# A linear-attention and FFN kernel on one core: all FFN2 pairs as seven block products, key-weight sums folded on TensorE, and a new order of parts

## The chip, the cores and the metric

The kernel runs on one core of a Trainium2 chip. Its time is the device time of one execution in microseconds (us). PE is TensorE, DVE is VectorE, ACT is ScalarE, POOL is GpSimd, and SP is SyncE, whose queue issues nearly all the DMAs of this kernel.

## The reference

All data are float32. x is 2048 x 512, there are 32 heads of 16, and the FFN is 1792 wide.

```python
x  = A_x
xn = _layernorm(x)                                  # no scale, no shift, eps 1e-5
q, k, v = split_heads(xn @ wqkv)
phi = lambda u: concat(softmax(u @ w_phi), softmax(-(u @ w_phi)))   # per head, 16 -> 32
kv  = einsum("bhsf,bhsd->bhfd", phi(k), v);  z = phi(k).sum(over s)
o   = einsum(phi(q), kv) / (einsum(phi(q), z) + 1e-6)
s   = o @ wo
g   = silu(mish(xn @ w1 + b1) @ w2)
out = x + s * g
```

## The kernel before

**How it is ordered.** The kernel is written as named parts, and a table ORDER lists them: a letter for the kind of part and a number for its chunk. Running the parts only records operations, each with the engines that may do it and a price for each engine. `simulate`, a planner in Python that runs when the kernel is built, then places the recorded operations one after the other on DVE (V), POOL (G), ACT (A) and SP's queue (Q), by data, by free buffers of a pool and by prices; PE's operations stay in the order in which the parts recorded them. The chosen order is then issued by one helper, `issue`, so nearly every instruction of the trace carries its line (L372 before), and groups are told apart by their tiles. An `either` operation may go to DVE or POOL. The planner also counts a shared memory port of DVE and POOL (`port`), and it prices a DMA by its bytes over DRATE.

**How products are made.** Every float32 operand is split into a high and a low part of a rounded type (`split`: the high part is a rounding copy, the low part the difference), and a product is three matmuls: low by high, high by low, high by high. Large products are cut into 2 x 2 blocks and made by seven block products instead of eight, from sums and differences of blocks.

**Stages, in about the order of time.** `fold` multiplies the key and query weights by the per-head map w_phi: 4 matmuls of 128x128 for each of the 4 chunks of 128 rows (tiles wkf and wqf), which the profile shows as 8 records. `weights_k` and `weights_s` build the seven block operands of the joint key and value weights (wv0, wv1, wk, ws1 to ws4). Part N (`norm`) loads one tile of 128 rows of x, forms its mean and variance on DVE, adds eps, takes the power -1/2 on POOL (tile rs), scales, transposes on PE (tile pt) and writes the block operands (tiles fh, fl, xs, xc). Ka to Kd are the four parts of the seven key and value products of a chunk pair (banks kx, ky, kz); the value tiles are four fixed buffers v0 to v3, and A adds phi(k) v into kvp. Q makes the queries, D and U the quotient, O the product with wo. P splits one w1 block and writes it to DRAM (w1d), M loads it back (w1b), and L loads the block operands of the second half of the tokens (fh, fl from xd; 14 transfers of 512 KB). Fa to Fd are the seven products of FFN1 for one pair of 128 columns and half of the tokens; their outputs ha to hd go to DRAM (hd). R prepares w2. G (`ffn2`, `act`) is FFN2: for each T of eight groups of 256 tokens and each b of seven pairs of hidden chunks it loads the hidden block (tile r), takes Mish on ACT, splits it (ah, al) and adds its products into the banks y. For b under DIRECT = 2 that product is made directly: 12 matmuls of 512 columns, or in the last group 24 of 256. For b = 2 to 6 the block sums (three operations on r) come first, the split is of 128x896 instead of 128x512, and the product is 21 matmuls of 256 columns. E (`final`) joins the banks of a T (tile yy), takes Silu, and multiplies and adds s and x.

PE may use eight PSUM banks. The pools that the change touches: `s2` (11 buffers of 128x512: x, k, ha to hd, r and its splits for b under DIRECT, xx, sr), `slot` (38 of 128x1024) and `rq`.

Of the kernel before, what the change touches and what calls it, by code (L numbers as in the profile page):

```python
# [17 lines left out]
P = 128  # L18
# [15 lines left out]
SLOTS, S2 = 38,11  # L34
SLACK, AHEAD, LAT = 15000, 40000, 150
WAKE, NEAR = 13, 2500
ORDER = """
wk0 N6 N0 wv1 N1 wk1 wv0 N2 Ka0 Ka1 N3 ws Kb0 N7 b1 Kc0 N4 Kd0 wq0 wq1 N5 Kb1 P0 Kc1 Fa0 Kd1 A0 Ka2 Kb2 Kc2 Fb0 N8 N9
N10 Kd2 A1 Ka3 Kb3 Fc0 Kc3 N11 Kd3 N12 P5 A2 Ka4 Fd0 Kb4 Fa5 Fb5 Kc4 A3 N14 P4 Ka5 Fc5 Kd4 Kb5 Kc5 Fd5 N13 Fa4 Kd5 Fb4
A4 Fc4 N15 Ka6 Kb6 A5 Ka7 Kc6 Kb7 P3 P2 P6 Kc7 Kd7 Fa6 Kd6 Fa3 Fa2 Fb3 wQ Fb6 M0 Fc3 Fc6 Fd4 A6 P1 A7 Fa1 Fb2 Fd3 Q0  # L40
Fd6 Fc2 z D0 Fb1 Fc1 D1 L Q3 Q1 D2 Q2 Fa7 D3 Fb7 Fd1 Fd2 D4 M1 Q4 M3 Fc7 Fa10 Fd7 Fa8 D5 Fb8 D6 Fc8 M2 Fd8 D7 Fb10 Q7
M6 Fa9 D8 M5 Fc10 M4 Fb9 Q5 Fd10 Fc9 Q6 D9 Fa13 Fd9 Fa12 D10 Ub0 Fb13 Fb12 D11 Fc13 Fc12 D12 wo0 Fa11 wo1 Fb11 D13 Ua0
D14 Fc11 Fd13 O1 O4 O6 O7 R1 O0 O3 O5 R2 R0 Fd11 Fd12 G7 D15 Ua1 R4 G8 O2 Ub1 G14 G15 R5 O9 O15 O10 O8 G9 G16 R3 G17
G10 G11 R6 G12 G18 G19 G13 E1 G0 O14 G1 G20 E2 G2 O13 G3 G4 O11 G28 G5 G29 G30 G6 G31 G32 G33 G34 G35 E0 G21 G36 G22
G23 G24 E4 G37 G38 G39 G40 G41 G25 G42 G26 O12 E5 G27 G43 G44 G45 G49 E3 G46 G50 G47 G48 G51 E6 E7
# [8 lines left out]
class Program:  # L54
# [105 lines left out]
    def links(self):  # L160
        ops = self.ops
        wr, rd = {}, {}
        for o in ops:
            o.succ, dep = [], set()
# [27 lines left out]
    def simulate(self, at):  # L192
# [22 lines left out]
        dma = port = told = 0  # L215
# [25 lines left out]
        def go(o, e):  # L241
            nonlocal aset, dma, port, half, code, fetched, cold
# [31 lines left out]
            if e == "Q":  # L274
                if not lanes:
                    dur = 0
                    busy[e] = now
                nb = calls[0][1][0].free_size() * calls[0][1][0].shape[0] * 4
                dma = max(dma, now + (1100 if now > 2500 else 1350)) + nb / DRATE
                end = max(dma + 1000, now + 2000 + nb / 200)  # L280
                lanes.append(end)
                heapq.heappush(events, (dma - BACK, 2, -1))
# [16 lines left out]
        while left:  # L299
# [34 lines left out]
            for e in ("A", "V", "G", "Q"):  # L334
# [3 lines left out]
                while ready[e]:  # L338
# [4 lines left out]
                    if e in o.lock and port > now + PTOL:  # L343
# [16 lines left out]
                if held and port > told:  # L360
                    told = port
                    heapq.heappush(events, (port, 2, -1))
# [40 lines left out]
def block_kernel(ctx: ExitStack, tc: tile.TileContext, x, wqkT, wv, phi, wo, w1, b1, w2, out):  # L403
# [9 lines left out]
    for tag, n in (("slot", SLOTS), ("s2", S2), ("sm", 13), ("rq", 5), ("st", 3 * NT), ("tq", 2)):  # L413
        pools[tag] = ctx.enter_context(tc.tile_pool(name=tag, bufs=n))
        prog.cap[tag] = n
# [52 lines left out]
    mhalf = const.tile([P, 1], F32, name="mhalf")  # L468
    b1t = const.tile([P, FC], F32, name="b1t")
    bmask = const.tile([P, 8], F32, name="bmask")  # L470
    vb = [const.tile([P, D], F32, name=f"v{i}") for i in range(4)]
# [68 lines left out]

    def norm(t):
        xx = load_x(t)
        st = sm([P, 6], f"st{t}")
        V.bn_stats(st, xx)
        mv = alloc("st", [P, 2], f"mv{t}")
        V.bn_aggr(mv, st)
        rs = alloc("st", [P, 1], f"rs{t}")
        V.tensor_scalar(rs, mv[:, 1:2], 1e-5, None, op0=ALU.add)
        G.tensor_tensor(rs, rs, mhalf, op=ALU.pow)
        nb = alloc("st", [P, 1], f"nb{t}")  # L550
        V.tensor_scalar(nb, mv[:, 0:1], rs, -1.0, op0=ALU.mult, op1=ALU.mult)
        with one():
            V.tensor_scalar(xx, xx, mv[:, 0:1], rs, op0=ALU.subtract, op1=ALU.mult)
# [69 lines left out]
    ek, eq, rq, phT, oT, kv = {}, {}, {}, {}, {}, {}  # L623
# [10 lines left out]
    def kv_a(c):  # L634
        x, z, v0 = bank([P, D], f"kx{c}"), bank([P, D], f"kz{c}"), vb[2 * c % 4]
# [6 lines left out]
    def kv_b(c):  # L642
        x, y, v1, k1 = kv[c], bank([P, D], f"ky{c}"), vb[(2 * c + 1) % 4], s2(f"k{2 * c + 1}p")
# [6 lines left out]
    def kv_c(c):  # L650
# [5 lines left out]
        plus(vb[(2 * c + 1) % 4], y)  # L656
# [36 lines left out]
    def kv_acc(p):  # L693
# [101 lines left out]
    def prep2(b):  # L795
# [5 lines left out]
        if b < NB - 2:  # L801
            th, tl, eh, el = (slot([P, n, 2 * P], f"w2{m}{b}", F32R) for m, n in (("h", 4), ("l", 4), ("g", 3), ("m", 3)))
        else:
            w = alloc("tq", [P, 16, 2 * P], f"w2t{b}", F32R)
            th, tl, eh, el = w[:, 0:4], w[:, 4:8], w[:, 8:11], w[:, 11:14]
# [6 lines left out]
        split(e, eh, el, either)  # L812
        w2_[b] = [(th[:, i], tl[:, i]) for i in range(4)] + [(eh[:, i], el[:, i]) for i in range(3)]
# [120 lines left out]
    def final(T):  # L934
        y = lambda n: ys[T][HOME[T == NQ - 1][n][0]][:, HOME[T == NQ - 1][n][1], :]
        plus_ = lambda o, a, b: V.tensor_tensor(o, a, b, op=ALU.add)
        if T < NQ - 1:
# [13 lines left out]
            for i in range(2):  # L951
                t = token(T, 1 - i)
                xx, st = s2(f"xx{t}"), s2(f"sr{t}")
                Q.dma_start(xx, x[t * P:(t + 1) * P, :])
                Q.dma_start(st, sdram[t])
                either(st, u[:, i], st, op=ALU.mult)
                either(xx, st, xx, op=ALU.add)
                Q.dma_start(out[t * P:(t + 1) * P, :], xx)
# [23 lines left out]

    w = {"o": [None] * KC}
# [65 lines left out]
    def sums():  # L1049
# [16 lines left out]
        for i in range(4):  # L1066
# [46 lines left out]
```

## Time and profile before

| | |
|---|---|
| median of 3 runs | 501.36 us (500.89 to 501.74) |
| profiled execution, its own time | 501.55 us |
| its span, first to last instruction | 499.8 us |
| mean granted clock of TensorE | 0.991 |
| PE busy | 487.7 us, 98% |
| DVE busy | 443.6 us, 89% |
| ACT busy | 282.4 us, 57% |
| POOL busy | 271.1 us, 54% |
| DMA | 105.69 MB, mean 211 GB/s |

Busy time of an engine is given over the span. Matmuls are pipelined, so one is listed with 0.39 us where the next starts 0.23 us later: a step from start to start is what a matmul costs in a full row.

### The profile page before, as it was taken

How to read it: one execution, taken by the hardware profiler on the slowest of the kernel's cores; microseconds unless marked ns; L12 is line 12 of the kernel's file. 1: busy time of each engine (PE TensorE's matmuls, PEld its weight loads, DVE VectorE, ACT ScalarE, POOL GpSimd, SP SyncE). 2: the span in 40 equal slices, each digit the busy share in tenths (PEclk: the TensorE clock that was granted, in tenths of full speed). 3: DMA queues.
4: the chain of work that ended last, by engine and by line, in shares of the span. 5: the costliest groups of instructions: out<-in, count | busy, mean ns of one | idle time of the engine just before them, and what ended most of it. 6: DMA issues, size and time to landing. Idle time of an engine off the chain costs nothing.

```text
span 499.8 us, 10023 instructions
## 1 busy us (share of the span) xinstructions
PE 487.7 (98%) x3690; PEld 424.3 (85%) x3690; DVE 443.6 (89%) x830; ACT 282.4 (57%) x433; POOL 271.1 (54%) x204
## 2 busy tenths in 40 slices
PE   8699999999999999999999999999999999999996
PEld 8478888878888889888898878778998899999996
DVE  6989999989999999999999989989587899768875
ACT  4676666445365552535243664487356888758611
POOL 4669997689688154889559497643020312112200
PEclk9799999999999999999999999999999999999999
DMA  8524438646979879888766286462644846644742
GB/s 303 185 92 161 148 97 297 220 190 171 358 287 321 298 257 337 306 274 285 251 216 231 100 289 225 170 211 94 201 133 148 269 150 191 207 150 139 255 154 85
DMA packets 68641, 105.69 MB, mean 211 GB/s; under 512 B 6896, under 2 KB 37744, under 8 KB 68592
## 3 DMA queue, kind: packets, MB, share of 16 engines
q1 hardware_dynamic: 68448, 104.79, 62.1%
q8 instruction: 29, 0.48, 0.4%
q10 hardware_dynamic: 144, 0.26, 0.2%
q14 instruction: 20, 0.16, 0.1%
HBM read 60.60 MB, written 44.43 MB: 210 GB/s over the span
## 4 chain that ended last, share of the span: by engine, by line
PE 91%; DVE 6%; ACT 2%; issue 1%; DMA 0%; DVEq 0%; ACTq 0%
PE y L372 28%; PE fx L372 15%; PE pw L372 9%; PE kx L372 8%; PE fy L372 7%; PE qx L372 5%; PE ky L372 4%; PE fz L372 4%; PE qy L372 2%; PE pn L372 2%; PE kz L372 2%; PE kvp L372 1%; PE pt L372 1%; PE qz L372 1%; PE wake L372 1%; PE wqf L372 1%
## 5 line engine op out<-in xcount | busy, mean ns | idle before, releaser
L372 POOL TENSOR_TENSOR r<-r 128x128 f32<-128x128 f32 (+1 forms) x18 | 10.2, 576 | 95.3 <-DVE r L372 56.6
L372 ACT ACTIVATE ah<-r 128x896 fp32r<-128x896 f32 (+1 forms) x56 | 46.8, 854 | 18.0 <-DVE r L372 9.4
L372 DVE TENSOR_TENSOR al<-r,ah 128x896 fp32r<-128x896 f32 (+1 forms) x45 | 46.3, 1047 | 9.1 <-ACT ah L372 4.9
L372 DVE TENSOR_TENSOR r<-r 128x128 f32<-128x128 f32 (+1 forms) x102 | 36.2, 384 | 6.8 <-ACT r L372 5.1
L372 ACT ACTIVATE r<-r 128x512 f32<-128x512 f32 x56 | 34.1, 624 | 14.1 <-DMA r<-hd 12.4
L372 PE MATMUL y<-w2t,ah 128*128 128x256 f32 x224 | 41.0, 283 | 0.0
L372 PE MATMUL fx<-fh,w1b 128*128 128x512 f32 x112 | 38.5, 392 | 0.0
L372 PEld LDWEIGHTS y<-w2t,ah 128*128 128x128 f32 x224 | 34.9, 192 | 0.2
L372 PE MATMUL y<-w2t,al 128*128 128x256 f32 x112 | 31.7, 283 | 0.0
L372 POOL TENSOR_TENSOR al<-r,ah 128x896 fp32r<-128x896 f32 (+1 forms) x11 | 20.1, 1829 | 21.0 <-ACT ah L372 9.5
L372 PE MATMUL y<-w2h,ah 128*128 128x256 f32 x96 | 27.2, 283 | 0.0
L372 PE MATMUL y<-w2l,ah 128*128 128x256 f32 x96 | 27.2, 283 | 0.0
L372 PE MATMUL y<-w2h,al 128*128 128x256 f32 x96 | 27.1, 283 | 0.0
L372 PEld LDWEIGHTS fx<-fh,w1b 128*128 128x128 f32 x112 | 21.0, 188 | 5.0 <-DVE ha L372 0.4
L372 PE MATMUL fx<-fl,w1b 128*128 128x512 f32 x56 | 21.9, 390 | 0.0
L372 PEld LDWEIGHTS y<-w2t,al 128*128 128x128 f32 x112 | 21.5, 192 | 0.2
L372 ACT ACT_TABLE_LOAD x13 | 16.7, 1283 | 6.9 <-DVE yy L372 5.5
L372 PE MATMUL y<-w2g,al 128*128 128x256 f32 x72 | 20.4, 283 | 0.0
L372 PE MATMUL y<-w2m,ah 128*128 128x256 f32 x72 | 20.4, 283 | 0.0
L372 PE MATMUL y<-w2g,ah 128*128 128x256 f32 x72 | 20.4, 283 | 0.0
L372 PE MATMUL fy<-fh,w1b 128*128 128x512 f32 x56 | 19.5, 389 | 0.0
L372 ACT ACTIVATE hb<-fx,b1t 128x512 f32<-128x512 f32 x14 | 9.6, 689 | 17.0 <-PE fx L372 14.5
(735 smaller groups left out, 1837.8 us busy)
## 6 DMA issues: line engine op xcount, KB each, us to landing
r<-hd SPq DMA_DIRECT2D x56, 256.0 KB, 3.5
xd<-xc SPq DMA_DIRECT2D x8, 896.0 KB, 5.5
w1b<-w1d SPq DMA_DIRECT2D x14, 512.0 KB, 4.6
w1b<-w1d SPq DMA_DIRECT2D x14, 384.0 KB, 4.3
so<-so SPq DMA_DIRECT2D x16, 256.0 KB, 2.6
x<-x SPq DMA_DIRECT2D x15, 256.0 KB, 4.0
w1a<-w SPq DMA_DIRECT2D x7, 512.0 KB, 5.4
w1d<-w1sh SPq DMA_DIRECT2D x7, 512.0 KB, 2.8
```

Of the source, the lines that this page charges most:

```text
L372: ins = getattr(e, m)(*a, **k)
```

## The change

- **FFN2.** DIRECT goes from 2 to 0, so that b = 0 and 1 take the path of the seven block products in all eight groups T. Their hidden blocks move from pool s2 to pool slot. For b = 0 to 4 one of the two weight tiles is laid out anew, one of its halves in s2.
- **Key weights.** Before, wkr kept the fold of chunks 0 and 1, and DVE added the fold of chunks 2 and 3 to it. Now `sum_k` folds chunk 0 and chunk 2 into one bank (and 1 and 3 into another), which is the sum; `low_k` folds chunks 2 and 3 and splits them at once; `diff_k` folds 0 and 1 and subtracts them from the value weights; `last_k` makes the fourth sum. Eight chunk folds stand where four stood.
- **Layer norm.** From tile 2 on, eps and power are taken once for two tiles (`stats`), so the first of a pair waits for the second's statistics.
- **Buffers.** The value tiles come from s2, which grows from 11 to 15 buffers; rq grows from 5 to 8.
- **Output.** The last multiplication and addition of `final` become a part of their own, H.
- **Planner.** One port clock for DVE and another for POOL, with a gap of GUARD = 140 behind DVE; PEN goes from -1000 to 0; DRATE from 300 to 400, with more for short runs; NEAR from 2500 to 4000; an operation also follows the first one on the same pooled tile.
- **Order.** ORDER is written anew.

```diff
-DIRECT = 2
+DIRECT = 0
-PEN, HOLD, MARGIN, PTOL = -1000, 300, 1000, 0
-BACK, COLD, DRATE, LANES, SWITCH = 1500, 3400, 300, 8, 300
+PEN, HOLD, MARGIN, GUARD = 0, 300, 1000, 140
+BACK, COLD, DRATE, LANES, SWITCH = 1500, 3400, 400, 8, 300
-SLOTS, S2 = 38,11
+SLOTS, S2 = 38,15
 ORDER = """
-wk0 N6 N0 wv1 N1 wk1 wv0 N2 Ka0 Ka1 N3 ws Kb0 N7 b1 Kc0 N4 Kd0 wq0 wq1 N5 Kb1 P0 Kc1 Fa0 Kd1 A0 Ka2 Kb2 Kc2 Fb0 N8 N9
+N0 kl wv1 wv0 kd N2 N1 N8 Ka1 wq0 N3 Ka4 ks N9 N6 k4 N7 Ka0 N4 Kb0 N5 Kc0 Kd0 Ka3 Kb1 N10 Kc1 P0 N11 Kb3 Kd1 Ka5 b1
...
-    def fold(wT, name, c):
-        ps = bank([P, D], f"{name}f{c}")
+    def fold(wT, name, *cs):
+        ps = bank([P, D], f"{name}f{cs[0]}{len(cs)}")
         with one():
-            for g in range(KC):
-                PE.matmul(ps[:, g * P:(g + 1) * P], wT[c][:, g, :], phit[:, g, :], start=True, stop=True)
+            for c in cs:
+                for g in range(KC):
+                    PE.matmul(ps[:, g * P:(g + 1) * P], wT[c][:, g, :], phit[:, g, :], start=c == cs[0] and g == 0,
+                              stop=c == cs[-1] and g == KC - 1, skip_group_check=True)
...
+    def stats(ts):
+        n = len(ts)
+        rs = alloc("st", [P, n], f"rs{ts[0]}")
+        mv = alloc("st", [P, n, 2], f"mv{ts[0]}")
+        for i, t in enumerate(ts):
+            xx = load_x(t)
+            st = sm([P, 6], f"st{t}")
+            V.bn_stats(st, xx)
+            V.bn_aggr(mv[:, i], st)
+            xs_[t] = xx, mv[:, i, 0:1], rs[:, i:i + 1]
+        V.tensor_scalar(rs, mv[:, :, 1], 1e-5, None, op0=ALU.add)
+        G.tensor_tensor(rs, rs, mhalf[:, 0:n], op=ALU.pow)
...
-        x, z, v0 = bank([P, D], f"kx{c}"), bank([P, D], f"kz{c}"), vb[2 * c % 4]
+        x, z = bank([P, D], f"kx{c}"), bank([P, D], f"kz{c}")
+        v0 = vs[2 * c] = s2(f"v{2 * c}")
...
-            ps = fold(wkT, "wk", 2 + j)
-            V.tensor_tensor(s[:, j], wraw["k"][:, j], ps, op=ALU.add)
-            split(ps, hi[:, j], lo[:, j])
...
+    def sum_k():
+        wraw["s"], wkv[3] = slot([P, 2, D], "ws2"), halves("ws", 1)
         for j in range(2):
+            ps = fold(wkT, "wk", j, j + 2)
+            V.tensor_tensor(wraw["s"][:, j], ps, wraw["v", 0][:, j], op=ALU.subtract)
+            split(ps, *(t[:, j] for t in wkv[3]))
+        wkv[4] = split_raw(wraw["s"], "ws2")
+    def low_k():
+        wkv[2] = halves("wk", 1)
+        for j in range(2):
+            split(fold(wkT, "wk", 2 + j), *(t[:, j] for t in wkv[2]))
```

PE at the start of the program. Before, the first folds come first, and the products kx and kz of two chunk pairs follow (x is a tile of the input, pt its transpose, wkf a fold):

```order
L372 MATMUL wake<-ones 128x128 x13
L372 MATMUL wkf_144<-phit,wkT_139 128x128 x4
L372 MATMUL wkf_145<-phit,wkT_140 128x128 x4
L372 MATMUL pt_151<-ident,x_146 128x128 x4
L372 MATMUL pt_157<-ident,x_152 128x128 x4
L372 MATMUL pt_166<-ident,x_161 128x128 x4
L372 MATMUL wkf_172<-phit,wkT_141 128x128 x4
L372 MATMUL wkf_173<-phit,wkT_142 128x128 x4
L372 MATMUL pt_182<-ident,x_177 128x128 x4
L372 MATMUL kx_183<-wv0h,fl_106 128x512
L372 MATMUL kx_183<-wv0l,fh_105 128x512
```

In the changed kernel:

```order
L371 MATMUL wake<-ones 128x128 x13
L371 MATMUL pt_144<-ident,x_141 128x128 x4
L371 MATMUL wkf_147<-phit,wkT_137 128x128 x4
L371 MATMUL wkf_148<-phit,wkT_138 128x128 x4
L371 MATMUL wkf_156<-phit,wkT_135 128x128 x4
L371 MATMUL wkf_157<-phit,wkT_136 128x128 x4
L371 MATMUL pt_167<-ident,x_162 128x128 x4
L371 MATMUL pt_173<-ident,x_170 128x128 x4
L371 MATMUL pt_183<-ident,x_178 128x128 x4
L371 MATMUL kx_185<-wv0h,fl_102 128x512
```

The four folds that stood apart now stand together behind one transpose. Further down, behind the products of two chunk pairs and two query folds, PE has the summed folds, two transposes whose x comes late, and then the third pair:

```order
L371 MATMUL wkf_202<-phit,wkT_135 128x128 x4
L371 MATMUL wkf_202<-phit,wkT_137 128x128 x4
L371 MATMUL wkf_203<-phit,wkT_136 128x128 x4
L371 MATMUL wkf_203<-phit,wkT_138 128x128 x4
L371 MATMUL pt_207<-ident,x_180 128x128 x4
L371 MATMUL pt_217<-ident,x_212 128x128 x4
L371 MATMUL pt_222<-ident,x_214 128x128 x4
L371 MATMUL kx_225<-wv0h,fl_102 128x512
```

The summed folds put two chunks into one bank, twice; the kernel before has no such rows.

SP's queue where L's loads (fh, fl) are issued while PE makes the queries and FFN1 of the second half. Before, the last of them and the first reloads of w1 (w1b) behind them:

```order
L372 DMA fh_580<-xd 128x1024
L372 DMA fl_581<-xd 128x1024
L372 DMA fh_578<-xd 128x1024
L372 DMA fl_579<-xd 128x1024
L372 DMA fh_582<-xd 128x1024
L372 DMA fl_583<-xd 128x1024
L372 DMA fh_576<-xd 128x1024
L372 DMA fl_577<-xd 128x1024
L372 DMA fh_584<-xd 128x1024
L372 DMA fl_585<-xd 128x1024
L372 DMA w1b_660<-w1d_444 128x768
L372 DMA w1b_661<-w1d_445 128x768
```

In the changed kernel, the same stretch of L's loads:

```order
L371 DMA w1b_621<-w1d_350 128x768
L371 DMA kvw<-kvd 32x4x256
L371 DMA w1b_622<-w1d_351 128x768
L371 DMA fh_609<-xd 128x1024
L371 DMA hd_577<-hc_573 128x512
L371 DMA fl_610<-xd 128x1024
L371 DMA hd_577<-hb_572 128x512
L371 DMA fh_615<-xd 128x1024
L371 DMA fl_616<-xd 128x1024
L371 DMA w1b_623<-w1d_352 128x1024
L371 DMA w1b_624<-w1d_353 128x1024
L371 DMA fh_613<-xd 128x1024
```

The reloads of w1 were behind all of L's loads and now stand among them.

PE in FFN2, the first group and pair b = 0 (y are the banks, w2 the weights). Before, the first of 12 direct matmuls:

```order
L372 MATMUL y_858<-w20h,al_0_857 128x512
L372 MATMUL y_858<-w20l,ah_0_856 128x512
L372 MATMUL y_858<-w20h,ah_0_856 128x512
L372 MATMUL y_858<-w20h,al_0_857 128x512
L372 MATMUL y_858<-w20l,ah_0_856 128x512
L372 MATMUL y_858<-w20h,ah_0_856 128x512
```

In the changed kernel, the first of the 21 matmuls of the block products ("x2" are two of one name that follow each other):

```order
L371 MATMUL y_877<-w2h_843,al_0_876 128x256
L371 MATMUL y_877<-w2l_844,ah_0_875 128x256
L371 MATMUL y_877<-w2h_843,ah_0_875 128x256
L371 MATMUL y_877<-w2g_845,al_0_876 128x256
L371 MATMUL y_877<-w2g_845,ah_0_875 128x256 x2
L371 MATMUL y_878<-w2g_845,al_0_876 128x256
L371 MATMUL y_878<-w2g_845,ah_0_875 128x256 x2
L371 MATMUL y_878<-w2h_843,al_0_876 128x256
```

The columns of a matmul are halved, and the weights w2g and w2m are operands that b = 0 did not have.

## Rows read from the trace of the kernel before

**Rows 1.** The page: busy time of the engines, and the chain that ended last.
```profile
PE 487.7 (98%) x3690; PEld 424.3 (85%) x3690; DVE 443.6 (89%) x830; ACT 282.4 (57%) x433; POOL 271.1 (54%) x204
...
PE 91%; DVE 6%; ACT 2%; issue 1%; DMA 0%; DVEq 0%; ACTq 0%
```

**Rows 2.** Windows: stretch, length, busy PE PEld DVE ACT POOL, clock, DMA share, GB/s.
```profile
40.00:340.00 300.00, 299.92 (x2416) 249.96 (x2415) 282.69 (x513) 157.66 (x254) 221.10 (x151) 1.00 0.69 237
...
0.00:40.00 40.00, 32.45 (x176) 27.68 (x177) 33.23 (x83) 25.61 (x47) 25.01 (x31) 0.91 0.54 187
330.00:495.00 165.00, 165.00 (x1260) 154.06 (x1259) 135.98 (x252) 107.85 (x152) 30.64 (x32) 1.00 0.52 169
...
20.00:26.00 6.00, 4.82 (x11) 3.84 (x12) 5.88 (x12) 1.98 (x4) 4.09 (x4) 0.50 0.02 4
...
40.00:60.00 20.00, 20.00 (x150) 16.31 (x149) 19.56 (x43) 13.76 (x23) 18.72 (x20) 1.00 0.44 155
```

**Rows 3.** Waits of PE, whole span: who waited for whom, us, times, longest.
```profile
PE kx L372 <- DVE wkl L372: 3.1, 1, 3.1
PE pt L372 <- ACT x L372: 2.2, 3, 1.1
PE wake L372 <- DVE mhalf L478: 1.1, 1, 1.1
PE kx L372 <- POOL wv0l L372: 1.0, 1, 1.0
```

**Rows 4.** Timeline of PE at the start: start, us, instruction, idle before and releaser.
```profile
21.18 0.77 PE L372 MATMUL kx<-wv0h,fl 128*128 128x512 f32 x1 [3.10 <-DVE wkl L372]
...
22.17 0.63 PE L372 MATMUL kx<-wv0h,fh 128*128 128x512 f32 x1
22.60 0.63 PE L372 MATMUL kx<-wv0h,fl 128*128 128x512 f32 x1
...
31.96 0.40 PE L372 MATMUL kx<-ws3h,fh 128*128 128x512 f32 x1
32.19 0.40 PE L372 MATMUL kx<-ws3h,fl 128*128 128x512 f32 x1
```

**Rows 5.** The chain of waits, 0 to 45 us: start, us, what.
```profile
6.71 0.91 PE wkf L372 x8
...
36.26 3.57 PE wqf L372 x32
39.83 0.44 PE pt L372 x4
40.27 1.39 PE kx L372 x6
```

**Rows 6.** DMA from 0 to 16 us: GB/s in 40 slices of 0.4 us.
```profile
GB/s 0 0 0 0 37 204 265 287 390 364 353 282 333 353 364 358 328 333 328 384 384 394 405 405 384 389 410 410 405 405 410 410 399 410 410 405 405 405 410 410
```

**Rows 7.** Timeline of PE in FFN2: 512-column matmuls, and 256-column ones.
```profile
319.93 0.39 PE L372 MATMUL y<-w20l,ah 128*128 128x512 f32 x1
320.15 0.39 PE L372 MATMUL y<-w20h,ah 128*128 128x512 f32 x1
...
488.34 0.28 PE L372 MATMUL y<-w2h,al 128*128 128x256 f32 x1
488.46 0.28 PE L372 MATMUL y<-w2l,ah 128*128 128x256 f32 x1
```

**Rows 8.** Groups by tile and form, 315 to 500 us: busy, mean ns, idle before.
```profile
L372 DVE TENSOR_TENSOR al<-r,ah 128x896 fp32r<-128x896 f32 x33 | 38.7, 1181 | 9.1 <-ACT ah L372 4.9 <-PE y L372 4.1
...
L372 DVE TENSOR_TENSOR r<-r 128x128 f32<-128x128 f32 x68 | 23.5, 366 | 1.7 <-POOL r L372 1.0
...
L372 DVE TENSOR_TENSOR r<-r 128x256 f32<-128x256 f32 x34 | 13.9, 419 | 5.1 <-ACT r L372 5.1
...
L372 DVE TENSOR_TENSOR al<-r,ah 128x512 fp32r<-128x512 f32 x12 | 8.1, 679 | 0.0
```

**Rows 9.** DMA from 180 to 215 us, and two windows in it (columns as in rows 2).
```profile
DMA packets 3783, 10.57 MB, mean 302 GB/s; under 512 B 421, under 2 KB 933, under 8 KB 3780
...
193.00:197.00 4.00, 4.00 (x34) 3.91 (x33) 3.97 (x12) 1.15 (x3) 1.45 (x1) 1.00 1.00 363
...
205.00:209.00 4.00, 4.00 (x19) 3.31 (x18) 4.00 (x6) 2.17 (x4) 4.00 (x5) 1.00 1.00 363
```

More of the change, by code (lines that the diff above doesn't have):

```diff
@@ L161, in links @@
         ops = self.ops
-        wr, rd = {}, {}
+        wr, rd, head = {}, {}, {}
         for o in ops:
-            o.succ, dep = [], set()
+            o.succ, dep = [], {head.setdefault(n, o.idx) for n in o.tiles if self.tag.get(n, "ps") != "ps"}
             for n in o.reads:
@@ L265, in go @@
             if e in o.lock:
-                dur += max(0, port - now)
-                port = now + dur
+                port["V"], port["G"] = now + dur, now + dur + (GUARD if e == "V" else 0)
             o.start, o.eng = now, e
@@ L277, in go @@
                     busy[e] = now
-                nb = calls[0][1][0].free_size() * calls[0][1][0].shape[0] * 4
-                dma = max(dma, now + (1100 if now > 2500 else 1350)) + nb / DRATE
-                end = max(dma + 1000, now + 2000 + nb / 200)
+                dma = max(dma, now + (1100 if now > 2500 else 1350)) + volume(calls[0][1]) / DRATE
+                end = dma + 1150
                 lanes.append(end)
@@ L342, in simulate @@
                         continue
-                    if e in o.lock and port > now + PTOL:
+                    if e in o.lock and port[e] > now:
                         held = True
@@ L387, in locks, with volume @@
     return aps[0].free_size() > 1 if m in ("tensor_scalar", "tensor_copy") else len(aps) > 2
+def volume(aps):
+    runs = []
+    for v in aps[:2]:
+        n = 1
+        for st, c in reversed(list(v.ap)):
+            if st != n:
+                break
+            n *= c
+        runs.append(n)
+    return aps[0].free_size() * aps[0].shape[0] * (4 if min(runs) > 128 else 4.7)
 def bcast(a):
@@ L467, in block_kernel @@
     ones = const.tile([P, P], F32, name="ones")
-    mhalf = const.tile([P, 1], F32, name="mhalf")
+    mhalf = const.tile([P, 2], F32, name="mhalf")
     b1t = const.tile([P, FC], F32, name="b1t")
     bmask = const.tile([P, 8], F32, name="bmask")
-    vb = [const.tile([P, D], F32, name=f"v{i}") for i in range(4)]
     nc.vector.memset(ones, 1.0)
@@ L539, in load_x @@
         return xx
-    def norm(t):
[L542 to L549, printed above, removed]
+    xs_ = {}
+    def stats(ts):
[10 more added lines that the diff above has]
+        G.tensor_tensor(rs, rs, mhalf[:, 0:n], op=ALU.pow)
+    def norm(t):
+        if t not in xs_:
+            stats((t,) if t < EACH else (t, t + 1))
+        xx, mean, rs = xs_.pop(t)
         nb = alloc("st", [P, 1], f"nb{t}")
-        V.tensor_scalar(nb, mv[:, 0:1], rs, -1.0, op0=ALU.mult, op1=ALU.mult)
+        V.tensor_scalar(nb, mean, rs, -1.0, op0=ALU.mult, op1=ALU.mult)
         with one():
-            V.tensor_scalar(xx, xx, mv[:, 0:1], rs, op0=ALU.subtract, op1=ALU.mult)
+            V.tensor_scalar(xx, xx, mean, rs, op0=ALU.subtract, op1=ALU.mult)
             A.activation(xx, xx, AF.Identity, bias=nb, scale=rs)
@@ L811, in prep2 @@
         split(t, th, tl, either)
-        split(e, eh, el, either)
-        w2_[b] = [(th[:, i], tl[:, i]) for i in range(4)] + [(eh[:, i], el[:, i]) for i in range(3)]
+        w2_[b], i = [(th[:, i], tl[:, i]) for i in range(4)], 0
+        for hi, lo in es:
+            n = hi.shape[1]
+            split(e[:, i:i + n], hi, lo, either)
+            w2_[b] += [(hi[:, j], lo[:, j]) for j in range(n)]
+            i += n
     hd, w1d, part = {}, {}, {}
@@ L950, in final @@
             A.activation(u, u, AF.Silu)
[L951 to L958, printed above, removed]
+            ys[T] = u
             return
@@ L980, in final, with gate @@
             Q.dma_start(out[at], xx)
+    def gate(T):
+        for i in range(2):
+            t = token(T, 1 - i)
+            xx, st = s2(f"xx{t}"), s2(f"sr{t}")
+            Q.dma_start(xx, x[t * P:(t + 1) * P, :])
+            Q.dma_start(st, sdram[t])
+            either(st, ys[T][:, i], st, op=ALU.mult)
+            either(xx, st, xx, op=ALU.add)
+            Q.dma_start(out[t * P:(t + 1) * P, :], xx)
     w = {"o": [None] * KC}
```

73 lines of the change are left out of this document (35 added, 38 removed).

## The prediction

> **What bounds the kernel now.** I read the page's shares and its chain first: PE is busy for 98% of the span and is 91% of the chain that ended last, DVE 6% [rows 1]. Then the windows, to see where the rest lies: from 40 to 340 us PE is busy for 299.92 of 300 us, from 330 to 495 us for all 165.00, but in the first 40 us only for 32.45 [rows 2]. So behind 40 us the time is the sum of PE's steps, an idle engine is worth nothing there, and a new order can only lose there. Only the start has something to give. PE's waits say what: 7.4 us in all, of which 3.1 is one wait of kx for DVE's wkl, 2.2 are transposes that wait for ACT's scaled x, 1.0 is a low part of the value weights from POOL, and 1.1 is the very first instruction [rows 3]. The timeline shows what the 3.1 us cost beside themselves: behind it 12 matmuls start 0.43 us apart (22.17, 22.60), where others start 0.23 apart (31.96, 32.19) [rows 4]. The granted clock of 20 to 26 us is 0.50, the lower level of 1.2 GHz, against 1.00 later [rows 2]; what PE did ahead of it was to be idle for those 3.1 us. The slow steps cost 12 x 0.20 = 2.4 us more.
>
> The sum goes by the profiled execution: 501.55 us, of which 499.8 is span and 1.75 lies around it. The median is 0.19 lower.
>
> **FFN2 matmuls, on the path: -3.6 us.** A 512-column step is 0.225 us (319.93 to 320.15 and the like; over twelve it is 0.227), a 256-column step 0.12 [rows 7]. For groups T = 0 to 6 and b = 0, 1 (14 products) 12 x 0.227 = 2.72 becomes 21 x 0.12 = 2.52: -0.20 each, -2.8. In the last group 24 x 0.12 = 2.88 becomes 2.52, twice: -0.7. PE has no wait in this stage, so all of it is on the path as long as the operands keep coming (below). The Trainium skill, "TensorE: Matmul & The Clock Gate", section "Back-to-back issue gap", gives an isolated matmul N/2.4 + 2.5 ns from start to start: 215.8 and 109.2 ns. By it the saving would be an estimated 4.8 us; the trace's steps are 5 and 10% longer, and the measured ones decide.
>
> **Key-weight folds, on the path: +3.6 us.** Four more chunk folds. Four of the query's take 3.57 us [rows 5], so +3.6. They take the place of the two DVE additions and two ACT copies of wkr, which is no gain on PE by itself. The two large terms cancel; the rest decides.
>
> **The start: -2.8 us, between 0 and -4.2.** As far as the second chunk pair's kx with the ws2 operands, before starts it at 40.27 [rows 5]; from the end of the wake matmuls at 6.7 [rows 5] this is 33.6 us, with 22.9 of matmuls at full clock by their steps, and 10.7 lost (2.4 of it to the clock). For the changed kernel I laid its own order of PE over the durations and landings of the rows, up to the third pair's kx with ws2, which has 21.0 us of matmuls ahead of it. The losses that I find: 0.4 for the first x; 1.65 at the fourth fold, whose weights are the eleventh load of SP and come with the first 3.4 MB, at about 11.8 us by the sum of the GB/s row [rows 6]; 1.3 at the third transpose, whose x waits on ACT behind the split of the value weights; 0.4 for the first low part; 0.35 at the next transpose; 1.05 and 0.25 at the two transposes behind the summed folds; 0.5 at the third kx, for the low part of ws; 0.3 behind it. That is 6.2, against 10.7 before, and 0.3 more for what such a chain forgets: -4.2. The wait of 3.1 goes because `low_k` splits its folds at once, so the bank comes free; next late is the fourth fold's load. But between 10.25 and 15.9 us PE has only some 2.3 us of work, and a stretch with little work on PE stood ahead of the fall of the clock in the trace before. If the clock falls to the lower level again for as long as there, 2.4 to 2.7 us go back, and 1.5 is left. I take the middle of 4.2 and 1.5. If DVE, which is busy for 33.23 of the first 40 us [rows 2] and serves this stretch in another order, is late as before, nothing is left: the other end, 0.
>
> **The reloads among L's loads: +0.4 us, between 0 and +6.4.** Two waits are moved: the w1b reloads stand now between the fh and fl loads, so a late fl delays all that is behind it on SP's one queue, and FFN1's first products of the second half wait for both. Between the places on PE which before has at about 182 and 213 us, 12 transfers of 512 KB of L, four reloads of 512 KB, four of 384 KB and five writes of hd must pass: 11.3 MB in 31 us, 364 GB/s. Before moved 10.57 MB in 35 us there, 302 GB/s on average; in windows with the engines fully busy it moved 363 [rows 9]. At 302 GB/s they take 37.4 us, 6.4 too long; at 363 they are on time to 0.1. I am near the second row, since this queue is full for the whole stretch.
>
> **DVE in FFN2: +0.2 us, between 0 and +11.** 16 products more need block sums and the larger split. By the two programs' instructions DVE gets 33 more r of 128x128 (12.1 us by 366 ns each), 16 more r of 128x256 (6.7), 15 more al of 128x896 (17.7), and 12 al of 128x512 fewer (-8.1) [rows 8], and `final` has 7 additions of 256 columns in place of 512 (-1.8): +26.6 us. DVE's busy time in 330 to 495 us is 135.98 of 165 [rows 2], so 162.6 of about 161.4 is wanted. This fits only if DVE does part of it earlier. It can: hidden blocks of many pairs are loaded and split ahead in the order, and at no place in it does the sum of DVE's durations up to a product reach PE's time. From 40 to 340 us DVE is busy for 282.69 of 300, 94%, and still PE has no wait [rows 2]; if 94% is the most that can be had, 162.6 need 172.6, and PE is 11 us late. ACT (107.85 of 165, and about 5 more) and POOL have room.
>
> **At nothing.** Pairs of tiles in the layer norm take seven POOL powers and seven DVE additions away, off the path; they hold the first tile of a pair until the second is loaded, which is in the chain of the start. The value tiles in s2, rq, and w2 in another pool only change when buffers come free: PE has no wait behind 40 us that they could take away, and one that they added would be of the size of rows 3, about 1 us. H moves the last additions of a group later on DVE, SP and POOL; nobody waits for the output but the end. The tail behind the last matmul at about 495 us is the same operations.
>
> **Sum.** -3.6 + 3.6 - 2.8 + 0.4 + 0.2 = -2.2 us: 499.35 by the profiled execution, 499.2 by the median.
>
> **The rivals.** About 0.2% (1.0 us) is what a measurement of this kernel can tell from no change.
> - *The start gives nothing* (chance 0.20): the clock falls, or DVE's order is late, so the new folds eat what the wait gave. For it: DVE is busy for 5.88 of 6 us from 20 to 26 [rows 2]. Against it: the longest wait has lost its cause. Without the -2.8 the sum is +0.6, less up to 0.7 of the start: 501.3.
> - *The start gives all* (0.16): the clock stays at 1.00 and the waits are those that I found. -4.2 for -2.8, and no burst cost: 497.4.
> - *The loads are late, slower* (0.11): at the mean rate of 302 GB/s PE stands at FFN1's products of the second half, up to 6.4 us. It decides below about 336 GB/s, where 2.6 us are lost (11.3 MB in 33.6 us) and the gain is gone. With 4.5, the middle between that and the end, for the 0.4: 503.3. Against it: the full windows of rows 9.
> - *DVE becomes the bound in FFN2, slower* (0.10): it decides once DVE comes 2.4 us late, so that the gain is gone. Between 1.2 late (162.6 against 161.4) and 11.2; the middle is 6.2, for the 0.2: 505.2. For it: 162.6 is more than the stage. Against it: ACT's Mish and the loads run ahead, and DVE's idle time of before, 29 us, is almost all in short waits for ACT that a longer queue fills.
> - *DVE and POOL exclude each other* (0.03): if operations of DVE and POOL that read memory could not run side by side, FFN2 would need 162.6 + 30.64 = 193 us of the pair, 32 more than PE: up to 531. Before, 135.98 + 30.64 = 166.6 just fills 165, which doesn't refute it in this stage; but from 40 to 60 us the two are busy for 19.56 and 18.72 of 20 us [rows 2], which does for the mix there. The rule that an operation of DVE with two inputs in SBUF shuts out a GpSimd operation that reads it is in the Trainium skill, "SBUF — State Buffer", section "Who interferes with whom"; the blocks r and their splits are of this kind, the bank reads of 40 to 60 us in part are not.
>
> **How the numbers follow.** The forecast as summed has a chance of 0.40 and by itself reaches from 498.2 to 500.3. With *all of the start* (0.16) it makes faster 0.56; *nothing from the start* is the same, 0.20; loads, DVE and the exclusion make slower 0.24. The range reaches down to 496.8, below 497.4 by the uncertainty of the chain, and up to 503.5, which takes in late loads at their middle and leaves out most of the two DVE cases.
>
> **What will show it.** Right: PE idle in the first 40 us falls from 7.5 to some 5, no row of a wait of kx for wkl, the first kx with ws2 operands near 34 us; y has only 256-column rows, 0.12 apart; PE busy for the whole of FFN2. Wrong: a granted clock near 0.50 in the windows from 10 to 30 us; PE waits for w1b, fh or fl between 180 and 215; waits of y for al in FFN2, DVE there busy for all of the time. A wait that starts anywhere else between 40 and 300 us, where the order is new and before had none, would also make this wrong, by its own length.

## The result, and the profile after

The changed kernel takes 502.69 us (median of 20 runs, 500.13 to 508.37) where the kernel before, run beside it, takes 500.36 (20 runs, 499.09 to 501.99). The ratio is 1.0043, interval 1.0026 to 1.0060: slower by 0.4%, some 2.2 us. The ratio leaves out two executions of the changed kernel in a slower state, 507.64 and 508.37 us. The forecast was 499.2 and faster; the time lies in its range (496.8 to 503.5), its sign is wrong. The profiled execution of the changed kernel took 501.77 us, span 499.9.

The page's busy times and shares of the chain, to be set beside [rows 1]:

```profile
PE 485.1 (97%) x3842; PEld 428.0 (86%) x3842; DVE 456.0 (91%) x883; ACT 287.3 (57%) x440; POOL 266.2 (53%) x199
...
PE 82%; DMA 7%; DVE 7%; issue 2%; ACT 1%; POOL 1%; SPq 0%; DVEq 0%; POOLq 0%
```

DMA has come into the chain that ended last: 7%, against 0% before. The waits of PE over the whole span (who waited for whom, us, times, longest) say where:

```profile
PE pt L371 <- ACT x L371: 3.0, 2, 1.8
PE wkf L371 <- DMA wkT<-wqkT: 1.7, 2, 1.4
PE fx L371 <- DMA w1b<-w1d: 1.3, 1, 1.3
PE wake L371 <- DVE mhalf L489: 1.1, 1, 1.1
PE pt L371 <- DVE wsl L371: 1.0, 1, 1.0
PE y L371 <- DVE yc L371: 0.7, 1, 0.7
PE fy L371 <- DMA fl<-xd: 0.7, 1, 0.7
PE kx L371 <- DVE wsl L371: 0.5, 1, 0.5
PE kx L371 <- ACT wqf L371: 0.2, 1, 0.2
```

The 3.1 us for wkl [rows 3] are gone. Three waits are new and lie behind 40 us, where PE had none: for w1b, for fl, and for yc. The windows (columns as in [rows 2]) show the start, the stretch of L's loads, and FFN2:

```profile
0.00:40.00 40.00, 32.25 (x200) 27.70 (x201) 33.37 (x93) 27.05 (x51) 21.48 (x27) 1.00 0.58 195
180.00:215.00 35.00, 34.34 (x190) 29.72 (x189) 33.42 (x58) 17.67 (x28) 27.59 (x19) 1.00 0.97 332
...
330.00:495.00 165.00, 164.34 (x1340) 159.71 (x1331) 150.94 (x307) 114.25 (x157) 26.65 (x23) 1.00 0.55 182
```

The start runs at the upper clock level (1.00 for 0.91) and is still no busier: 32.25 us for 32.45. In FFN2 DVE went from 135.98 to 150.94 us, and PE lost 0.66.

**Work and lost time, apart.** A busy PE doesn't tell a step of 0.23 us from one of 0.43. So over all matmuls of a trace I added up the time from each start to the next beyond the usual step of its kind (0.227 us for 512 columns, 0.120 for 256, 0.111 for a record of a fold, 0.109 for a transpose). It holds the waits and the slow steps. What is left of the time is PE's work and the two ends:

| trace, its time | lost in all | 0 to 40 us | 200 to 240 | 460 to 500 | elsewhere | time less lost |
|---|---|---|---|---|---|---|
| before, 501.55 | 16.9 | 10.5 | 0.5 | 0.0 | 5.9 | 484.7 |
| before, a second trace, 499.61 | 14.9 | 8.8 | 0.5 | 0.0 | 5.5 | 484.7 |
| changed, 501.77 | 17.0 | 8.1 | 3.1 | 0.9 | 5.0 | 484.8 |
| changed, a second trace, 503.35 | 18.5 | 7.4 | 6.0 | 0.0 | 5.0 | 484.9 |

How large the sums at the start are depends on what counts as the usual step of the smaller matmuls, wake's among them; the differences between the traces do not. So the work is the same to 0.2 us, and the difference lies in the waits: less at the start, more between 200 and 240 us.

### The profile page after: what moved, and what is told of

It is laid out like the page before. It is cut to its first block, busy times and chain, and to the rows that moved or that the text cites. A ratio compares the mean times of both kernels' runs of the same rounds, so it can differ in the third digit from the quotient of the medians.

```text
span 499.9 us, 10373 instructions
## 1 busy us (share of the span) xinstructions
PE 485.1 (97%) x3842; PEld 428.0 (86%) x3842; DVE 456.0 (91%) x883; ACT 287.3 (57%) x440; POOL 266.2 (53%) x199
## 4 chain that ended last, share of the span: by engine, by line
PE 82%; DMA 7%; DVE 7%; issue 2%; ACT 1%; POOL 1%; SPq 0%; DVEq 0%; POOLq 0%
PE y L371 21%; PE fx L371 15%; PE pw L371 9%; PE kx L371 9%; PE fy L371 7%; PE ky L371 4%; PE fz L371 4%; PE qx L371 3%; PE pn L371 2%; DMA r<-hd 2%; DMA fl<-xd 2%; PE kz L371 2%; DVE al L371 2%; DMA w1b<-w1d 2%; PE kvp L371 2%
## 5 line engine op out<-in xcount | busy, mean ns | idle before, releaser
L371 ACT ACTIVATE ah<-r 128x896 fp32r<-128x896 f32 x56 | 51.2, 944 | 13.7 <-DVE r L371 9.7
L371 DVE TENSOR_TENSOR al<-r,ah 128x896 fp32r<-128x896 f32 x48 | 52.6, 1123 | 3.0 <-ACT ah L371 2.4
L371 PE MATMUL y<-w2h,al 128*128 128x256 f32 x160 | 45.5, 284 | 0.7 <-DVE yc L371 0.7
L371 PE MATMUL y<-w2h,ah 128*128 128x256 f32 x160 | 45.3, 283 | 0.0
L371 PE MATMUL y<-w2l,ah 128*128 128x256 f32 x160 | 45.3, 283 | 0.0
L371 PEld LDWEIGHTS y<-w2h,al 128*128 128x128 f32 x160 | 30.7, 192 | 1.5 <-DVE yc L371 0.9
L371 PEld LDWEIGHTS y<-w2l,ah 128*128 128x128 f32 x160 | 30.7, 192 | 0.2
L371 PEld LDWEIGHTS y<-w2h,ah 128*128 128x128 f32 x160 | 30.7, 192 | 0.0
L371 POOL TENSOR_TENSOR al<-r,ah 128x896 fp32r<-128x896 f32 x8 | 17.0, 2130 | 22.7 <-DVE sr L371 18.6
L371 PEld LDWEIGHTS y<-w2g,ah 128*128 128x128 f32 x160 | 24.9, 192 | 0.0
```

Source lines behind the costliest of these rows:

```text
L371: ins = getattr(e, m)(*a, **k)
```

## The experiments

In these, M3 and M5 are the parts that reload blocks 3 and 5 of w1, and al is the low part of a split hidden block.

**Both kernels once more.** A second trace of each, with 12 runs.

> The changed kernel unaltered, for a second trace and the clock of each run. Theory A (loads): PE waits again for w1b and fl between 200 and 235 us, 1 to 4 us in all, and these waits differ from run to run by about as much as the times do. Theory B (start): the waits for loads are the 2.0 us of the first trace, and what differs between runs is the granted clock, with a lower one in runs that are 2 us longer. Both: a median near 502.7 us against 500.4 before.

> The kernel before, unaltered, for a second trace of it. If the first trace was typical: again 7.4 us of waits of PE, nearly all ahead of 40 us, with the 3.1 us wait for wkl and 12 steps at the lower clock behind it. If the clock falls only in some executions, this one has the wait but not the slow steps, and is about 2.4 us shorter than the first trace.

The changed kernel took 501.62 us beside 500.40, ratio 1.0022 (0.9998 to 1.0046); the kernel before took 500.37 beside 499.67, 1.0002 (0.9984 to 1.0020). In the second trace of the changed kernel the first product that uses the reloaded block 3 (timeline of PE: start, us, instruction, idle before and releaser):

```profile
232.47 0.80 PE L371 MATMUL fx<-fh,w1b 128*128 128x512 f32 x1 [2.87 <-DMA w1b<-w1d]
...
234.34 0.63 PE L371 MATMUL fx<-fl,w1b 128*128 128x512 f32 x1
234.77 0.63 PE L371 MATMUL fx<-fh,w1b 128*128 128x512 f32 x1
```

The wait is 2.87 us where the first trace has 1.34 at the same place, and behind it the matmuls start 0.43 us apart. In the second trace of the kernel before, the start:

```profile
21.07 0.47 PE L372 MATMUL kx<-wv0h,fl 128*128 128x512 f32 x1 [3.12 <-DVE wkl L372]
...
21.84 0.39 PE L372 MATMUL kx<-wv0h,fl 128*128 128x512 f32 x1
22.07 0.40 PE L372 MATMUL kx<-wv0l,fh 128*128 128x512 f32 x1
```

The same wait as in [rows 4], but behind it the steps are 0.23 us. The slow steps of the first trace are not part of the kernel: they come in some executions. Of 84 further executions of the kernel before (one of 968.8 us left aside), 28 had a mean granted clock of 0.991 or 0.992 and took 501.1 to 502.3 us; the other 56 had 0.994 or more and took 498.9 to 500.8. The trace that the prediction was made from, at 0.991, was one of the first kind.

**Order of the reloads.** Why does w1b come late? In the changed kernel's SP timeline (start, us, instruction, count) and its chain of waits (start, us, what), the reloads:

```profile
218.11 0.32 SPq L371 DMA_DIRECT2D w1b<-w1d  x1
219.00 0.32 SPq L371 DMA_DIRECT2D hd<-hc  x1
219.47 1.74 SPq L371 DMA_DIRECT2D w1b<-w1d  x3
...
222.20 1.28 SPq L371 DMA_DIRECT2D w1b<-w1d  x2
```

```profile
223.16 8.48 DMA w1b<-w1d
231.64 0.04 issue
231.68 1.65 PE fx L371 x6
```

The pair at 222.20 belongs to block 3, which PE uses at 231.68: the later one lands at 231.64. The four from 218.11 to 220.9 are block 5's, used first at 240 to 243, 14 to 16 us after they have landed. ORDER names M5 ahead of M3, and the planner takes a transfer's due time from its part's place there. The edit exchanges the two:

```diff
-... L M4 Fa11 M5 D3 Fc6 D4 M3 D5 ...
+... L M4 Fa11 M3 D3 Fc6 D4 M5 D5 ...
```

> The changed kernel with two names of ORDER exchanged (the reload of w1 block 3 is listed ahead of that of block 5, as they are used); only SP's queue differs. Theory A: the wait of fx for w1b of 1.34 us goes, the wait of fy for fl of 0.66 us stays: 1.3 us or more faster than the changed kernel, about 501.3. Theory B: no change of the median, 502.7. If the loads are just late as a whole, the wait moves to the next w1b by as much, 502.7 too.

500.32 us, ratio 0.9993 (0.9976 to 1.0010), 1.3 us less than the changed kernel in the same comparison (the means of the 12 executions each are 500.2 and 501.9). Its waits behind 40 us:

```profile
PE y L371 <- DVE yc L371: 0.8, 1, 0.8
PE fy L371 <- DMA fl<-xd: 0.3, 1, 0.3
```

The wait for w1b is gone, with the same bytes and the same instructions on DVE, ACT and POOL. By the table's measure 1.2 us are lost between 200 and 240, for 3.1 and 6.0.

An obvious doubt is that PE came to this place later here, since this trace lost 10.1 us at the start, for 8.1 and 7.4. The traces of the kernels below settle it. The changed kernel's two and three others without the exchange wait 0.7 to 2.9 us for block 3; the five with it don't (two kernels whose plan is new from the start are left aside). At like losses at the start (7.4 us in three traces) 6.0 us are lost between 200 and 240 without the exchange, slow steps among them, and 1.3 and 2.5 with it. So the cause of this wait is the order of the queue. The exchange doesn't make all loads early: an earlier PE still waits for others.

**FFN2 without the change.** DIRECT back to 2; the order on PE, DVE, ACT and POOL is the same up to about 295 us.

```diff
-DIRECT = 0
+DIRECT = 2
-... E2 G49 H2 E7
+... E2 G49 G50 G51 H2 E7
```

> The changed kernel with only the FFN2 change undone (DIRECT = 2; up to about 310 us every engine has the same order). If PE bounds FFN2, it loses the 3.6 us that the block products save and wins the wait of 0.7 us for yc: about 505.6. If DVE bounds FFN2 in the changed kernel, taking 26.6 us from it makes this 502.7 or faster.

504.81 us, ratio 1.0069 (1.0049 to 1.0090): 3.2 us over the changed kernel. Its time less the lost time is 488.2, for 484.8: 3.4. Its window of FFN2:

```profile
330.00:495.00 165.00, 165.00 (x1246) 153.69 (x1219) 129.39 (x258) 104.04 (x147) 26.68 (x19) 1.00 0.51 171
```

DVE has 129.39 us there, for 150.94; both fit. So the block products bring some 3.3 us, nearly all of the 3.6 that they were summed at.

**Half of the summed folds left out.** The sums are made of chunks 2 and 3 alone, so the operands made of them lack chunks 0 and 1. DVE, ACT and POOL do the same in the same order; PE has 16 matmuls of 128 columns fewer, 1.78 us.

```diff
+                if o.part == "ks" and o.eng == "PE":
+                    if i < 4:
+                        continue
+                    k = {**k, "start": i == 4}
```

> The changed kernel with half of the summed folds left out (the folds of chunks 0 and 1 in the two sums, 2 of the 4 extra chunk folds; the sums are then only of chunks 2 and 3). If the folds lie on the path as the sum had them, 0.89 us each, it is 1.8 us faster than the changed kernel, 500 to 501, with the same waits behind it. If the waits behind them (DVE's wsl, 1.0 and 0.5 us) do not depend on the folds, they grow by what is left out and the time stays.

503.59 us, ratio 1.0074 (1.0044 to 1.0104): not faster. The work is 1.7 us less (483.1 for 484.8). The folds lie between the first products of the second and the third chunk pair. PE's timeline of the changed kernel, and then of this one:

```profile
22.28 0.50 PE L371 MATMUL kx<-wv0h,xc 128*128 128x512 f32 x1 [0.24 <-ACT wqf L371]
...
32.07 0.47 PE L371 MATMUL kx<-wv0h,fl 128*128 128x512 f32 x1 [0.47 <-DVE wsl L371]
```

```profile
21.98 0.50 PE L375 MATMUL kx<-wv0h,xc 128*128 128x512 f32 x1 [0.23 <-ACT wqf L375]
...
29.57 1.28 PE L375 MATMUL pt<-ident,x 128*128 128x128 f32 x8 [0.64 <-DVE wsl L375]
...
31.66 0.77 PE L375 MATMUL kx<-wv0h,fl 128*128 128x512 f32 x1 [0.81 <-DVE wsl L375]
```

From the one product to the other it is 9.79 us in the changed kernel, 9.77 to 9.80 in all seven traces that have its start, and 9.68 here. The wait of kx for wsl, 0.5 us in the changed kernel, is 0.8 here, and two are new ahead of it (0.9 for v, 0.3 for xs). Of 1.78 us of PE only 0.1 arrive: this stretch goes by DVE. Why the kernel as a whole became slower is not settled. Its trace loses 11.9 us at the start, and has a stop of 1.9 us at 290.9 that the profile puts down to nothing (`issue`), far from the edit.

**One fold each, made into a sum on DVE.** This was to undo the second part: DVE adds in place of the summed folds.

```diff
+            V.tensor_tensor(wraw["s1"][:, j], wraw["k"][:, j], ps, op=ALU.add)
```

> The changed kernel with the four extra folds undone: the folds of chunks 2 and 3 are kept by a copy and added on DVE, the rest of the order stays. If PE bounds the start once it is under way, it wins 3.6 us: about 499.1. If the operands bound it (DVE and ACT, which get two additions and two copies more), PE waits for them as much longer: 502 to 503.

522.6 us (median of six, one of them 2625.74), ratio 1.0437 (1.0400 to 1.0474). It is no clean undo: with other operations the planner lays out all engines anew. Its largest wait, and the row of POOL behind it:

```profile
PE pt L371 <- ACT x L371: 14.2, 3, 11.5
```

```profile
100.75 1.56 POOL L371 TENSOR_TENSOR rs<-rs,mhalf 128x2 f32<-128x2 f32 x2 [5.14 <-DVE zacc L371]
```

A power of the layer norm stood behind a POOL operation that waited for DVE, and PE stood for 11.5 us at 91 us. What the folds are worth is not told by it.

**A power for every tile.** EACH = 16 in place of 2, with the exchange of M3 and M5.

> As swap_m, with eps and power of the layer norm taken per tile again, as before (9 powers more on POOL). If holding the first tile of a pair until the second is loaded costs PE at the start, the waits of pt for x (2.2 us there) shrink by about 1 us: 499.3. If the power per pair is at nothing, as the prediction had it: 500.3, within 0.3.

524.0 us, ratio 1.0475 (1.0447 to 1.0503), and again all is laid out anew: PE waits 6.4 us once for q11p and 4.6 once for v. This leaves open what the pairs are worth.

**The end of FFN2.** The wait for yc, from DVE's timeline of the changed kernel:

```profile
469.89 7.29 DVE L371 TENSOR_TENSOR al<-r,ah 128x896 fp32r<-128x896 f32 x7
477.10 0.42 DVE L371 TENSOR_TENSOR yc<-yy,y 128x256 f32<-128x256 f32 x1
```

DVE splits seven hidden blocks in a row, some for products that come later, and only then reads the bank that PE waits to reuse. A first edit, a slack of 0 for these reads in the planner, again with M3 and M5 exchanged:

> As swap_m (reload of w1 block 3 listed ahead of block 5), and in `final` the reads of the banks y get slack 0 in the planner, so that DVE reads a group's banks ahead of the splits al of the last group. If the wait of y for yc (0.7 us) is an order on DVE and not DVE's lack of time, it goes and no other comes: 0.5 to 0.8 faster than swap_m, about 499.6. If DVE is the bound at the end of FFN2, PE waits for al in its place: 500.3 or more.

504.65 us, ratio 1.0094 (1.0066 to 1.0122). The planner gave splits to POOL instead, and PE waited for those:

```profile
PE y L371 <- POOL al L371: 3.1, 2, 1.7
```

The second edit moves three single instructions after the planner has run (the exchange of M3 and M5 is kept): the reads of the banks go ahead of the last two al of the last group.

```diff
+        for o, at in ((2334, 464400), (2335, 464401), (2336, 464402)):
+            ops[o].start = at
```

> As swap_m (reload of w1 block 3 listed ahead of block 5), and on DVE the three reads of the banks of group 2 are put ahead of the last two splits al of the last group; every other place of every engine is kept. If the wait of y for yc (0.7 us) is only the order on DVE, it goes and nothing takes its place: swap_m less 0.5 to 0.8, 499.7 beside a swap_m of 500.3. If DVE lacks the time, PE waits for the two splits instead, 500.3 or more.

499.1 us, ratio 0.9984 (0.9969 to 0.9999). The wait is gone and no other came in its place in FFN2: DVE had room there, and only its order was late. In the time it can't be told apart from the exchange alone (0.9993; the intervals overlap). At 208 to 211 us this trace waits 0.8 us for w1b of another block and 0.6 for fl.

**Two writes behind a load as well.** In SP's queue two hd writes go behind the fl load that PE waited for.

```diff
+        for o, at in ((872, 208249), (875, 208250)):
+            ops[o].start = at
```

> As ycfirst, and on SP two writes of hd that nobody needs for 20 us are put behind L's loads that PE waits for; nothing else moves. If the rest of the lateness is the queue's order, the wait of fy for fl (0.3 to 0.7 us) goes: 499.3. If the burst is late as a whole, the wait moves to a later load: as ycfirst.

499.42 us, ratio 0.9983 (0.9968 to 0.9999). Behind 40 us its trace has no wait of PE at all, and it loses 0.7 us between 200 and 240; beside the run before, the two writes make no difference that shows. The rate of the stretch, 180 to 232 us, in the second trace of the changed kernel and then in this one, there with the shorter stretch of L's loads ahead:

```profile
180.00:232.00 52.00, 49.22 (x292) 43.31 (x290) 48.92 (x92) 20.99 (x36) 39.36 (x25) 1.00 1.00 344
```

```profile
180.00:215.00 35.00, 35.00 (x194) 30.60 (x193) 34.16 (x59) 18.59 (x30) 26.97 (x19) 1.00 0.90 318
180.00:232.00 52.00, 52.00 (x306) 46.09 (x305) 49.51 (x92) 22.59 (x39) 38.62 (x24) 1.00 0.95 349
```

344 and 349 GB/s: nearly one rate, with PE idle for 2.8 us there or not at all.

**The start, by order.** Three instructions that make wsl and wsh move ahead on DVE and ACT, once on top of the last kernel and once on the changed kernel alone.

```diff
+        for o, at in ((135, 27313), (139, 27916), (138, 27749)):
+            ops[o].start = at
```

> As best, and in the start the two splits wsl of the summed folds go ahead of other work on DVE and ACT (three places moved). If PE's start is bound by DVE's order there, the waits for wsl (1.0 and 0.5 us) shrink to 0.2 or less, and with them the slow steps that followed in two traces: 1.3 to 2 us faster than best, 497.5 to 498. If DVE's sum of work binds, the next operand is late by as much: as best.

> The changed kernel with only the three places of the start moved (as in best2). Same two cases by themselves: 1.3 us or more faster than the changed kernel (500.4 to 501.4), or unchanged (501.6 to 502.7). The waits for w1b and fl stay, and grow by what PE comes earlier if the loads do not come earlier too: then unchanged, with the start's gain lost between 200 and 235 us.

499.68 us, ratio 0.9995 (0.9979 to 1.0012), and 503.57 us, ratio 1.0065 (1.0046 to 1.0084): no gain on either. The waits of the latter at the start:

```profile
PE pt L379 <- DVE wsl L379: 1.3, 1, 1.3
...
PE kz L379 <- DVE xs L379: 0.6, 1, 0.6
```

The wait of kx for wsl is gone, that of the transpose grew from 1.0 to 1.3, and one of kz for xs is new. The wait moves along DVE's row, as with the folds left out.

## Why the prediction was wrong

The step that failed is **the reloads among L's loads**: +0.4 us by the prediction, 2.6 and 5.5 by the two traces (3.1 and 6.0 lost, for 0.5). It is the rival *the loads are late*, which had a chance of 0.11; its time of 503.3 is near the 502.69 measured, in part by luck, since it counts on 2.8 us from the start. The stretch of L's loads, 180 to 215 us, moved 332 GB/s, between the two rates that I weighed, and by my own formula 11.3 MB at 332 take 34.0 us, 3.0 more than there were. But the rate was the wrong question. The kernel with the two writes moved has 318 there by its window and PE doesn't wait, and over the longer stretch the rates agree (344 and 349). I summed the bytes between two places on PE and let them all be due at the end. What decides is who lands when within the queue: block 5 with 14 us to spare stood ahead of block 3 with none. The wait for block 3 ends at 231.68 us, behind the 180 to 215 us in which I had said that a wait for loads would show. The order of SP's queue was to be had before the run; I laid it over the landings for the start, and not here.

**The start**: -2.8 forecast, some -1 measured. In sum the waits are those that I found in its order: my losses made 6.2 and 0.3, and the waits at the start without wake's make 6.4 (3.0, 1.7, 1.0, 0.5 and 0.2). But the first product with ws2 operands, which I had near 34 us, starts later. PE's timeline of the changed kernel:

```profile
35.56 0.48 PE L371 MATMUL kx<-ws2h,fl 128*128 128x512 f32 x1
```

Seven traces have this start: the changed kernel's two and those of five kernels that differ from it only later. In them this product starts between 34.88 and 37.60 us (mean 35.8), and the three latest have slow steps ahead of it. The other side was too large as well. Of the 10.7 that the kernel before lost, 2.4 were slow steps that only a third of its executions have; by the table its two traces lose 10.5 and 8.8 between 0 and 40 us, weighted by a third and two thirds 9.4. The seven lose 8.1, 7.4, 10.1, 8.9, 7.4, 7.4 and 8.9 there, mean 8.3. One trace was taken for the kernel, and the kernel before is 0.2% faster by its later runs (500.36 for 501.36).

**FFN2's matmuls**: -3.6 forecast, 3.2 by the times and 3.4 by the traces of the kernel with DIRECT = 2. The steps stay what they were in [rows 7]; PE's timeline of the changed kernel:

```profile
477.80 0.28 PE L371 MATMUL y<-w2l,ah 128*128 128x256 f32 x1
477.91 0.28 PE L371 MATMUL y<-w2h,ah 128*128 128x256 f32 x1
```

The formula of the Trainium skill, "TensorE: Matmul & The Clock Gate", section "Back-to-back issue gap", gave an estimated 4.8 us. The trace does not agree: its steps are longer (0.227 and 0.120 us for 0.216 and 0.109), and the 3.2 to 3.4 us measured are near the 3.6 that follow from them.

**The folds**: +3.6 of work, right, since time less lost is the same to 0.2 with -3.6 and +3.6 in it. That all of it is on the path was wrong taken alone: with two of the four chunk folds in the sums left out, 0.1 of 1.78 us came through. In my sum this did no harm, because the start's losses were found with the folds in place; folds and waits of the start are one term, not two.

**DVE in FFN2**: +0.2 forecast, 0 to 0.9 measured. It didn't become the bound: DVE is busy for 150.94 us of 165, where I had 162.6. The counts came as I had them (101 r of 128x128, 50 r of 128x256 and 48 al of 128x896 on DVE); the prices were too high. Two groups of the changed kernel, to be set beside [rows 8]:

```profile
L371 DVE TENSOR_TENSOR al<-r,ah 128x896 fp32r<-128x896 f32 x48 | 52.6, 1123 | 3.0 <-ACT ah L371 2.4
...
L371 DVE TENSOR_TENSOR r<-r 128x128 f32<-128x128 f32 x101 | 29.3, 322 | 0.5
```

The mean of 366 ns for an r of 128x128 holds waits: in the trace before, 63 of the 68 take at most 0.30 us, and the five that run beside an operation of POOL take up to 2.20. By the means of those that run alone (286, 420 and 1086 ns) my sum gives 22.5 us for 26.6, and from the kernel with DIRECT = 2 to the changed one it is 21.6 (129.39 to 150.94). The other 6.6 us are what the new plan took out of this stage with the products as before (135.98 to 129.39). The loss was one wait of order, not of load.

*DVE and POOL exclude each other* didn't come, but single operations do exclude each other. Timelines of the changed kernel, an r on DVE alone and one beside POOL:

```profile
392.97 0.28 DVE L371 TENSOR_TENSOR r<-r 128x128 f32<-128x128 f32 x1
```

```profile
397.56 2.13 POOL L371 TENSOR_TENSOR al<-r,ah 128x896 fp32r<-128x896 f32 x1
397.64 2.20 DVE L371 TENSOR_TENSOR r<-r 128x128 f32<-128x128 f32 x1
```

The second r starts 0.08 us behind the al and ends just after it (399.84 and 399.69 us). The rule of the Trainium skill, "SBUF — State Buffer", section "Who interferes with whom", is that an operation of DVE with two inputs in SBUF contends with one of GpSimd that reads SBUF. The trace agrees, also in what is free: a yy<-yy,y of 128x256, which reads a bank, takes 0.41 to 0.42 us with POOL beside it (9 of 14) and without. A sum of busy times (150.94 and 26.65 of 165 us here, the 19.56 and 18.72 of 20 us of the prediction) can't refute it, because an operation that is held counts as busy. The stage didn't fill up because few such pairs meet: of 25.8 us in which both are busy there, 9.4 are of DVE operations with no bank among their inputs.

**At nothing**: no wait of PE was traced to the buffers or to H. What the pairs of the layer norm have in the start's waits for x is open.

Together: about -1 from the start, +2.6 to +5.5 between 200 and 240, 0 to +0.9 at the end of FFN2, and -0.7 elsewhere (5.0 for 5.7). That is +0.9 to +4.7, with +2.2 and +1.2 measured. With the order mended in two places the kernel takes 499.1 us, 0.16% less than the kernel before and about the time that was forecast. The time agrees by luck: the forecast was 2.2 us below a kernel before of 501.36, and this is 0.9 below one of 499.99. It is also under the 0.2% I called the least that can be told, and its interval just leaves 1 out.

Open: why three of the seven traces with the changed start have the lower clock there; the stop in the trace with half of the folds left out; the worth of the pairs of tiles and of the folds against DVE's additions.

## What to carry to other kernels

For a transfer in a full queue compare its own landing with its own first use, in the order of the queue; the bytes and the mean rate of the stretch say only whether somebody will be late. Take a second trace of the kernel that you start from before you count a loss in it as a gain to come. Where a planner lays out the instructions, undo a part by moving single instructions: a rebuilt plan can differ everywhere, and three of them here ended 5 to 24 us behind the kernel before. Price an operation of DVE by those that ran without POOL beside them: the mean of a group holds waits.

## What the hardware showed that was not expected

The same wait is followed by a lower clock in some executions and not in others. In the kernel before, PE idles 3.10 and 3.12 us for wkl, once with a granted clock of 0.50 behind it and once with steps at full speed. In the changed kernel's start, with waits of 0.5 to 1.8 us, three of seven traces have the lower clock between 28 and 40 us, at the same busy time (4.46 and 4.49 of 6 us); the window 28 to 34 us of the kernels with 499.1 and 499.42 us:

```profile
28.00:34.00 6.00, 4.46 (x25) 3.15 (x24) 5.69 (x15) 5.19 (x11) 5.20 (x4) 1.00 0.00 0
```

```profile
28.00:34.00 6.00, 4.49 (x24) 3.38 (x23) 5.59 (x15) 4.44 (x10) 5.20 (x4) 0.84 0.00 0
```

The time of the changed kernel scatters more: its 18 executions in the ratio spread over 5.8 us and the 12 of its second measurement over 5.6, for 2.9 of the kernel before and 3.5 with the reloads exchanged (12). The wait for w1b differs too, 1.34 and 2.87 us in its two traces. That the one makes the other is not shown: two kernels that keep this wait, DIRECT = 2 and the start by order alone, spread over 2.3 and 2.2 us in six executions each.
